# A two-branch attention kernel: three units of maxima, some weight casts and one value bank are moved

## The chip, the cores and the metric

The kernel runs on one core of a Trainium2 chip. The core has five engines that run side by side, each with its own queue that is worked through in order: TensorE (PE, matrix products; PEld is its loading of weights), VectorE (DVE), ScalarE (ACT), GpSimd (POOL) and SyncE (SP, which here issues all DMA transfers). Products land in PSUM, eight banks of 128 x 512 floats; everything else lives in SBUF or in device memory. The metric is device time of one execution, in microseconds (us); the profile numbers one execution from the start of its span.

## The reference, cut to what matters

The inputs are one sequence `x` of 2048 tokens with 448 features, and the weights of two attention branches with 16 heads of 28 features each.

```python
g = _sigmoid((x * gate_w).sum(-1, keepdims=True))
a = _A_ref(x, A_wqkv, A_w_phi, A_wo)
b = _B_ref(x, B_wqkv, B_wo)
return g * a + (1 - g) * b
```

Branch A is linear attention: queries and keys of each head are multiplied by `w_phi`, and their features are the softmax of the result beside the softmax of its negative. With `kv = phi_k^T v` and `z = sum(phi_k)`, the output is `(phi_q kv) / (phi_q z + 1e-6)`, times `wo`. Branch B is full softmax attention, `softmax(q k^T / sqrt(28)) v`, times its own `wo`.

## The kernel before, in words

Float32 products are made of rounded pieces: a tensor is kept as a high half (a cast on ScalarE) and a low half (raw minus high, on VectorE or GpSimd), and a product takes three passes: high by high, high by low, low by high. `split_weight` and `split_x` do the high half at once and put the low half into the list `lows`; `take_lows()` issues what is in that list. So the place of `take_lows()` sets where the low halves stand in VectorE's or GpSimd's queue. The order of each of PE, DVE, ACT and POOL is the order in which the code issues; only SP's queue is ordered by a scheduler.

The program has four parts.

Projection (iterations `n` = 4 to 19, about the first 63 us): `proj_qk` makes one 128 x 512 block of B's queries and keys in 11 passes, ScalarE and VectorE split it into `ev`, and SP writes it to memory (`qkd`). Here `x` is split (`XH`, `XL`), `wvA` is cast, and `fold` multiplies A's key weights by `w_phi`.

Key stage (`t` = 0 to 15, to about 181 us): for each 128 tokens A's key features (`pk`) and values (`pva`), and their product `pkv`.

Query stage (`q = i - 16`, from q = 0, about 181 to 324 us): for q up to 15, `pq` (11 passes), copied by ScalarE to `pcq`; `features1` takes minima and maxima on VectorE (`ext`), subtracts on POOL or VectorE (`featq`; for q = 4 and 6 the second subtraction, L431, is on VectorE) and ScalarE exponentiates; `features2` sums on VectorE and scales on POOL. Three iterations later `turn` transposes them on TensorE (`pft`) and ScalarE copies them to `fT`; every second iteration `numer` makes numerators and denominators (`pn`, copied to `oUa` on ScalarE). The normalization is spread over iterations: `normalize1` sends the denominators out by DMA (`dena`), `normalize2` takes the reciprocal on VectorE and sends it to memory and back, spread over the partitions (`rda`, then `rsa`), `normalize3` multiplies on VectorE (L400), `normalize4` casts to `oTa` (high on ScalarE, L408, low on POOL, L409). From q = 11 on, `out_a(t)` with t = q - 11 multiplies two `oTa` tiles by `woA` in 12 passes (`poa`), and `out_a2` scales by the gate (`ga`). `woA` itself is cast in this stage, high on ScalarE (L143), low on POOL (L144). From q = 18 on, `value_b` makes B's values (`pvb`).

Scores of B (about 363 us to the end): scores, exponentials and value products.

Spread over the first three parts are 80 *units of maxima*, `mx_unit()`: bounds of the scores of B's query rows. A unit is four matmuls of 28 rows into four PSUM banks (`pmd`, `pmb`), then twice a relu on ScalarE (L264) and a maximum on VectorE (L265, which the order calls ISA). Their banks form a ring of four (tag `mx`), so that a unit waits until the unit before it has been worked off by ScalarE (`pmd`) and VectorE (`pmb`). Units are numbered as they are issued; a few of them also ask for the next loads of rows (`qp`). In the query stage before, one stands in every iteration with q = 0, 1 and from 8 on, behind `pq`, and a second one in q = 19 to 25. Most other products take their bank from the ring `s` (four banks in the query stage, two from q = 22 on, where the maxima get six).

Of the kernel before, what the change touches and what calls it, by code (L numbers as in the profile page):

```python
# [17 lines left out]
P = 128  # L18
S = 2048
D = 448  # L20
# [3 lines left out]
NG = 4  # L24
# [17 lines left out]
def gated_mix_kernel(ctx, tc, xT, wqkB, wvB, wvA, wkAT, wqAT, phi, woA, woB,  # L42
# [7 lines left out]
    nc = tc.nc  # L50
# [56 lines left out]
    def run(dst, todo):  # L107
        for i, (l, r) in enumerate(todo):
            nc.tensor.matmul(dst, l, r, start=i == 0, stop=i == len(todo) - 1)  # L109
# [25 lines left out]
    lows = []  # L135

    def take_lows():
        while lows:
            lows.pop(0)()
# [98 lines left out]
    def mx_unit():  # L238

        u = mxs["u"]  # L240
        if u == NF:
            return
        mx_fin()
        mxs["u"] = u + 1
        gq, r = divmod(u, 16)
        g, qb = divmod(gq, NQ)
        c, qt = divmod(r, 4)
        hp, b = divmod(c, 2)
        col = 64 * gq + 16 * b + 4 * qt + 2 * hp
        if r in (4, 9) and gq + 1 < GM:  # L250
            pair_query(gq + 1, r // 9)
        if r == 4 and gq + 1 == GM:
            mx_query(GM)
        qc, kc = mxs[("qp", gq, hp)], mxs[("kp", g, c)]

        pm = [ps_mx(f"pm{'ddbb'[j]}{u}_{j % 2}") for j in range(4)]
        for j in range(4):
            i = (j + 2) % 4
            js = slice(32 * i, 32 * i + DH)
            nc.tensor.matmul(pm[j], qc[js, qt * P:(qt + 1) * P], kc[js, :], start=True, stop=True,  # L260
                             tile_position=(32 * i, 0))
        for i in range(2):
            rl = rlp.tile([P, 512], F32, tag="rl", name=f"rl{u}_{i}", bufs=psn[2])
            nc.scalar.activation(rl, pm[i], AF.Relu)  # L264
            nc.vector.tensor_tensor_reduce(rl, pm[2 + i], rl, 1.0, LOWEST, ALU.add, ALU.max,  # L265
                                           part[:, col + i:col + i + 1])
        if gq + 1 < GM and qt == 3 and qb == NQ - 1:
            pair_load(g + 1, c)
        if gq + 1 == GM and qt == 3:
            mx_load(GM // NQ, c)  # L270
        if r == 15:
            mx_reduce(gq)
# [53 lines left out]
    def split_x(t, raws):  # L326
        tt = slice(t * 512, (t + 1) * 512)
        if t == 3:
            for b, raw in enumerate(raws):
                nc.scalar.copy(XH[:, b, tt], raw)  # L330
                lows.append(lambda b=b, raw=raw: (nc.gpsimd if b == 2 else nc.vector).tensor_sub(
                    XL[:, b, tt] if b < 3 else XH[64:, 3, tt], raw[64 * (b == 3):],
                    f32(XH[64 * (b == 3):, b, tt])))
            return
        for b, raw in zip((0, 2), raws):
            nc.scalar.copy(XH[:, b:b + 2, tt], raw)

            def low(b=b, raw=raw):
                if b == 0:
                    nc.vector.tensor_sub(XL[:, 0:2, tt], raw, f32(XH[:, 0:2, tt]))  # L340
                else:
                    (nc.gpsimd if t > 1 else nc.vector).tensor_sub(
                        XL[:, 2, tt], raw[:, 0, :], f32(XH[:, 2, tt]))
                    nc.vector.tensor_sub(XH[64:, 3, tt], raw[64:, 1, :], f32(XH[64:, 3, tt]))

            lows.append(low)
# [66 lines left out]
    def out_passes(oT, c, w, g):  # L413
        tt = slice(c, c + P)
        return [(oT[:, 0, tt], w[:, 0, g, :]), (oT[:, 0, tt], w[:, 1, g, :]),
                (oT[:, 1, tt], w[:, 0, g, :])]
# [119 lines left out]
    def out_a(t):  # L536
        tb, tl = divmod(t, 2)
        po_of[t] = po = ps_s(f"poa{t}")
        run(po[:, :D], [x for g in range(NG)
                        for x in out_passes(oTs[tb][g % 2], g // 2 * 256 + tl * P, woA_s[:, :, :, :D], g)])  # L540

    def out_a2(t):
        ga = ta.tile([P, D], F32, tag="ga", name=f"ga{t}", bufs=3)
# [12 lines left out]
    def proj_qk(n, ev):  # L556

        m, t = UNITS[n]
        tt = slice(t * 512, (t + 1) * 512)
        pq = later.pop(0) if later else ps_s(f"pqk{t}_{m}")  # L560
        w, c = wB[m // 4], m % 4 * P
        run(pq, [(w[:, i, b, c:c + P], x) for b, x, i in x3(tt)])
        keep_qk(m, t, pq, ev)
# [30 lines left out]
    def splits(n):  # L594

        if n % 4 == 1 and n < 12:
            split_x(n // 4 + 1, raws.pop(("x", n // 4 + 1)))
        if n in (13, 15):
            split_part(wB[1], "wB1", 384, (n - 13) // 2)
        take_lows()  # L600
# [41 lines left out]
    for n in range(4, NP):  # L642
        take_acts()
        if n == 4:
            x_loads(2)
            raws[("x", 3)] = [load_last(b) for b in range(4)]
        if n == 8:
            nc.sync.dma_start(phi_s, phi)
            load_fold(wkAT, "k")
        if n == 10:  # L650
            part_loads("wB1", wqkB[:, :, 512:896], 384, "wB1")
        splits(n + 1)
        if n == 14:
            part_loads("wvA", wvA, 450, "wvA")
            nc.sync.dma_start(sel_s, sel)
            nc.sync.dma_start(mask_s, mask)
            for v in vap:
                nc.gpsimd.memset(v[:, :, 28:32], 0.0)
                nc.gpsimd.memset(v[:, :, 28:29], 1.0)
        if 16 <= n < 20:  # L660
            mx_unit()
        proj_qk(n, ev)
        if n in (17, 19):
            split_part(wvA_s, "wvA", 450, (n - 17) // 2)
            take_lows()
        if n in (13, 14, 15, 16):
            fold(wkA_s, "k", {13: 0, 14: 1, 15: 2, 16: 3}[n])
        if n == 10:
            pair_query(0, 0)
            pair_load(0, 0)  # L670
        if n == 15:
            pair_load(0, 1)
            pair_query(0, 1)
        if n in (14, 19):
            take_subs()
# [10 lines left out]
        return v  # L686

    def value_b(t, mid=None):
        pv = ps_s(f"pvb{t}")
        tok_major(pv, t, wvB_s, D, mid)  # L690
        nc.scalar.copy(vb[t // 8][:, t % 8, :, 0:DH], pv[:, :D].rearrange("p (h d) -> p h d", d=DH))

# [10 lines left out]
    for i in range(2 * NT + 11):  # L703
        t, q = i, i - NT
# [3 lines left out]
        if t < NT and t % 2 == 0:  # L708
            mx_unit()
            passes = (55 if t < NT - 4 else 44) + (4 if t >= 4 else 0)  # L710
            pace["n"], pace["at"] = 4 if t >= 4 else 0, [k * passes // 4 for k in range(1, 4)]
        if q in (0, 1):
            take_exps()
# [28 lines left out]
            fq[q - 1] = features2(fq[q - 1], f"q{q - 1}")  # L742
        if 0 <= q < NT:
            fq[q] = features1(pq, f"q{q}", nc.vector if q in (4, 6) else nc.gpsimd)
        if 0 <= t - 1 < NT - 1:
            fk[t - 1] = features2(fk[t - 1], f"k{t - 1}")
        if q in (0, 1) or q >= 8:
            mx_unit()
        if y >= 6 and y % 2 == 0 and tb - 3 < 8:
            num[tb - 3] = normalize2(ta, *num[tb - 3], f"a{tb - 3}", 2)  # L750
# [24 lines left out]
        if q == 2:  # L775
# [2 lines left out]
            for i in range(2):  # L778
                nc.sync.dma_start(raws["woA"][i], woA[:, 2 * i:2 * i + 2, :])
            part_loads("wvB", wvB, D, "wvB")  # L780
        if q in (4, 6):
            split_part(woA_s, "woA", D, (q - 4) // 2, nc.gpsimd)
        if q in (13, 15):
            split_part(wvB_s, "wvB", D, (q - 13) // 2)
        if q == 1:
# [458 lines left out]
```

## Time and profile before

| | us |
|---|---|
| three runs, median | 977.64 (976.87 to 979.13) |
| the profiled execution | 978.57 |
| its span (first to last instruction) | 976.8 |
| TensorE busy | 969.2 |
| ScalarE busy | 751.8 |
| VectorE busy | 715.7 |
| GpSimd busy | 227.8 |

The granted clock is 1.000 in the whole span. In a row of a timeline the first number is the start in us, the second the duration, then the engine, the line of the code, the operation, the tile written and those read, their shapes, and how often it was repeated; a bracket at the end is idle time of that engine ahead of it and what ended it. Matmuls overlap, so that the start of the next row, not the sum of the durations, gives TensorE's pace.

### The profile page before, as it was taken

How to read it: one execution, taken by the hardware profiler on the slowest of the kernel's cores; microseconds unless marked ns; L12 is line 12 of the kernel's file. 1: busy time of each engine (PE TensorE's matmuls, PEld its weight loads, DVE VectorE, ACT ScalarE, POOL GpSimd, SP SyncE). 2: the span in 40 equal slices, each digit the busy share in tenths (PEclk: the TensorE clock that was granted, in tenths of full speed). 3: DMA queues.
4: the chain of work that ended last, by engine and by line, in shares of the span. 5: the costliest groups of instructions: out<-in, count | busy, mean ns of one | idle time of the engine just before them, and what ended most of it. 6: DMA issues, size and time to landing. Idle time of an engine off the chain costs nothing.

```text
span 976.8 us, 22541 instructions
## 1 busy us (share of the span) xinstructions
PE 969.2 (99%) x8510; PEld 600.1 (61%) x8510; DVE 715.7 (73%) x1338; ACT 751.8 (77%) x1442; POOL 227.8 (23%) x236
## 2 busy tenths in 40 slices
PE   9999999999999999999999999999999999999998
PEld 8777877787777655555555555545555555555555
DVE  5567767788845678888888888888888888885112
ACT  4455655577865688989888898888988989887662
POOL 1135445577634800021001001011011011010010
PEclk9999999999999999999999999999999999999999
DMA  8873110023233333021132021122231222100441
GB/s 305 303 259 118 40 53 33 29 58 94 73 108 109 101 111 132 26 59 53 57 94 74 30 61 49 59 78 69 65 83 46 65 59 72 34 21 32 143 151 57
DMA packets 56140, 84.49 MB, mean 86 GB/s; under 512 B 17216, under 2 KB 23984, under 8 KB 56032
## 3 DMA queue, kind: packets, MB, share of 16 engines
q1 hardware_dynamic: 56032, 83.06, 27.1%
q8 instruction: 67, 1.10, 0.4%
q14 instruction: 41, 0.34, 0.1%
HBM read 54.86 MB, written 27.78 MB: 85 GB/s over the span
## 4 chain that ended last, share of the span: by engine, by line
PE 91%; DMA 5%; DVE 2%; ACT 1%; issue 1%; SPq 0%; DVEq 0%; ACTq 0%
PE g L863 29%; PE pv L1008 27%; PE pqk L109 4%; PE pk L127 4%; PE pva L127 4%; PE g L288 4%; PE poa L109 3%; PE pmd L260 3%; PE pob L109 3%; PE pq L109 3%; PE pvb L127 2%; PE pvb L109 2%; DMA rsa<-rda 2%; DMA qkd<-ev 1%; DMA xraw<-in_xT_dram 1%
## 5 line engine op out<-in xcount | busy, mean ns | idle before, releaser
L871 ACT ACTIVATE p<-g 128x512 f32<-128x512 f32 x1020 | 525.6, 608 | 82.7 <-PE g L863 82.4
L295 DVE TENSOR_REDUCE part<-g 128x1 f32<-128x512 f32 x704 | 442.3, 684 | 84.1 <-PE g L288 80.8
L863 PEld LDWEIGHTS g<-qst,kst 32*128 32x128 f32 x3060 | 220.9, 182 | 215.4 <-DVE part L295 195.1
L863 PE MATMUL g<-qst,kst 32*128 32x512 f32 x3060 | 337.6, 419 | 0.1
L1008 PE MATMUL pv<-p,vb 128*32 128x512 f32 x2048 | 273.0, 604 | 0.0
L288 PE MATMUL g<-kc,qc 28*128 28x512 f32 x704 | 233.3, 495 | 0.0
L265 DVE CUSTOM_DVE_ANT_0 rl<-pmb,rl 128x512 f32<-128x512 f32 x160 | 103.4, 683 | 49.6 <-ACT rl L264 49.6
L400 POOL TENSOR_TENSOR oUb<-oUb,rsb 128x512 f32<-128x512 f32 x15 | 19.3, 1289 | 489.9 <-DMA rsb<-rdb 366.2
L264 ACT ACTIVATE rl<-pmd 128x512 f32<-128x512 f32 x160 | 87.3, 601 | 31.1 <-PE pmb L260 29.3
L288 PEld LDWEIGHTS g<-kc,qc 28*128 28x128 f32 x704 | 86.2, 181 | 0.2
L1008 PEld LDWEIGHTS pv<-p,vb 128*32 128x32 f32 x2048 | 40.5, 108 | 66.2 <-issue 64.9
L109 PE MATMUL pqk<-XH,wB 128*128 128x512 f32 x192 | 59.4, 397 | 0.8 <-DVE ev L569 0.8
L568 ACT CAST ev<-pqk 128x512 fp32r<-128x512 f32 x28 | 16.0, 589 | 38.5 <-PE pqk L109 22.5
L1019 DVE SCALAR_TENSOR_TENSOR acc<-pob,gate,acc 128x448 f32<-128x448 f32 x12 | 8.2, 684 | 48.3 <-PE pob L109 48.3
L109 PE MATMUL poa<-woA_s,oTa 128*128 128x448 f32 x192 | 43.6, 375 | 0.0
L260 PE MATMUL pmb<-kp,qp 28*128 28x512 f32 x160 | 41.7, 495 | 0.4
L109 PEld LDWEIGHTS pqk<-XH,wB 128*128 128x128 f32 x192 | 35.3, 188 | 9.9 <-issue 1.5
L569 DVE TENSOR_TENSOR ev<-pqk,ev 128x512 fp32r<-128x512 f32 x28 | 18.9, 690 | 30.5 <-ACT ev L568 30.4
L260 PE MATMUL pmd<-kp,qp 28*128 28x512 f32 x160 | 39.9, 494 | 0.0
L127 PE MATMUL pk<-wkA_s,XH 128*128 128x448 f32 x128 | 39.4, 381 | 0.0
L109 PEld LDWEIGHTS poa<-woA_s,oTa 128*128 128x128 f32 x192 | 34.8, 188 | 6.6 <-issue 2.5
L109 PE MATMUL pq<-wqA_s,XH 128*128 128x448 f32 x128 | 37.3, 374 | 0.8 <-ACT oUa L381 0.8
(158 smaller groups left out, 1052.2 us busy)
## 6 DMA issues: line engine op xcount, KB each, us to landing
qkd<-ev SPq DMA_DIRECT2D x28, 512.0 KB
qst<-qkd SPq DMA_DIRECT2D x64, 112.0 KB
kst<-qkd SPq DMA_DIRECT2D x64, 112.0 KB
od<-oTb SPq DMA_DIRECT2D x48, 112.0 KB
rsa<-rda SPq DMA_DIRECT2D x8, 512.0 KB
oL<-od SPq DMA_DIRECT2D x8, 512.0 KB
rsb<-rdb SPq DMA_DIRECT2D x15, 256.0 KB
gad<-ga SPq DMA_DIRECT2D x16, 224.0 KB
```

The costliest lines, as they stand in the source:

```text
L109: nc.tensor.matmul(dst, l, r, start=i == 0, stop=i == len(todo) - 1)
L127: nc.tensor.matmul(dst[:, :n], l, r, start=i == 0, stop=i == len(todo) - 1, skip_group_check=True)
L260: nc.tensor.matmul(pm[j], qc[js, qt * P:(qt + 1) * P], kc[js, :], start=True, stop=True, tile_position=(32 * i, 0))
L264: nc.scalar.activation(rl, pm[i], AF.Relu)
L265: nc.vector.tensor_tensor_reduce(rl, pm[2 + i], rl, 1.0, LOWEST, ALU.add, ALU.max, part[:, col + i:col + i + 1])
L288: nc.tensor.matmul(pm, mxs[("qc", gq)][js, qt * P:(qt + 1) * P], mxs[("kc", gq // NQ, kb)][js, :], start=True, stop=True, tile_position=(3 ...
L295: nc.vector.tensor_reduce(part[:, col:col + 1], pm, AX.X, ALU.max)
L400: (nc.gpsimd if n == 1 else nc.vector).tensor_mul(oU, oU, rs)
L569: nc.vector.tensor_sub(e[:, 1, :], pq, f32(e[:, 0, :]))
L863: nc.tensor.matmul(st[j], kst_of[(gq // NQ, kt // 4)][js, k, (kt % 4) * P:(kt % 4 + 1) * P], qst_of[gq][js, q, :], start=n == 0, stop=n == ...
L871: nc.scalar.activation(p, st[j], AF.Exp, scale=SCALE)
L1008: nc.tensor.matmul(pv[32 * j:32 * j + 32, :], vb[kt // 8][:, kt % 8, 4 * g + j, :], pt[j], start=kt == 0, stop=kt == NT - 1, tile_position ...
```

## The change

Six small edits. In `split_x` the low half of the last block of `XH` goes to GpSimd. In iterations n = 16 to 19 the waiting low halves are issued behind the unit of maxima and ahead of the projection. The key stage issues them behind its first unit as well. `woA` is cast at the end of q = 3 and 4 instead of 4 and 6, and its first low half is issued within q = 4. The units of q = 8, 9 and 10 are left out there, and `out_a` issues one after its sixth pass for t = 1, 3 and 7 (q = 12, 14 and 18), so that from q = 19 on the numbers agree again. `value_b(4)`, the first after the banks are dealt out anew in q = 22, takes a bank of the maxima's ring; a bank of the ring `s` is passed over, so that the others stay where they were.

```diff
-                lows.append(lambda b=b, raw=raw: (nc.gpsimd if b == 2 else nc.vector).tensor_sub(
+                lows.append(lambda b=b, raw=raw: (nc.gpsimd if b > 1 else nc.vector).tensor_sub(
...
-        run(po[:, :D], [x for g in range(NG)
-                        for x in out_passes(oTs[tb][g % 2], g // 2 * 256 + tl * P, woA_s[:, :, :, :D], g)])
+        todo = [x for g in range(NG)
+                for x in out_passes(oTs[tb][g % 2], g // 2 * 256 + tl * P, woA_s[:, :, :, :D], g)]
+        for i, (l, r) in enumerate(todo):
+            if i == 6 and t in (1, 3, 7):
+                mx_unit()
+            nc.tensor.matmul(po[:, :D], l, r, start=i == 0, stop=i == len(todo) - 1,
+                             skip_group_check=True)
...
-        splits(n + 1)
+        if n < 16:
+            splits(n + 1)
...
         if 16 <= n < 20:
             mx_unit()
+            take_lows()
         proj_qk(n, ev)
         if n in (17, 19):
             split_part(wvA_s, "wvA", 450, (n - 17) // 2)
-            take_lows()
...
-        pv = ps_s(f"pvb{t}")
+        if t == 4:
+            ps_s("pvb_none")
+        pv = (ps_mx if t == 4 else ps_s)(f"pvb{t}")
...
             passes = (55 if t < NT - 4 else 44) + (4 if t >= 4 else 0)
+            take_lows()
...
+        if q == 4:
+            take_lows()
...
-        if q in (0, 1) or q >= 8:
+        if q in (0, 1) or q >= 11:
             mx_unit()
...
-        if q in (4, 6):
-            split_part(woA_s, "woA", D, (q - 4) // 2, nc.gpsimd)
+        if q in (3, 4):
+            split_part(woA_s, "woA", D, q - 3, nc.gpsimd)
```

On VectorE, iterations n = 17 and 18, before (`rl2` are the two maxima of unit 2, `ev` a projection's low half):

```order
L569 TENSOR_TENSOR ev1_4_586<-pqk1_4_574,ev1_4_586 128x512
L144 TENSOR_TENSOR wvA_s_116<-wvA_raw0_448,wvA_s_116 128x900
L265 ISA rl2_0_600,part_92<-pmb2_0_594,rl2_0_600 128x512
L265 ISA part_92 128x1
L265 ISA rl2_1_603,part_92<-pmb2_1_595,rl2_1_603 128x512
L265 ISA part_92 128x1
L569 TENSOR_TENSOR ev2_4_618<-pqk2_4_606,ev2_4_618 128x512
```

The same place after:

```order
L574 TENSOR_TENSOR ev1_4_586<-pqk1_4_574,ev1_4_586 128x512
L265 ISA rl2_0_599,part_92<-pmb2_0_593,rl2_0_599 128x512
L265 ISA part_92 128x1
L265 ISA rl2_1_602,part_92<-pmb2_1_594,rl2_1_602 128x512
L265 ISA part_92 128x1
L144 TENSOR_TENSOR wvA_s_116<-wvA_raw0_448,wvA_s_116 128x900
L574 TENSOR_TENSOR ev2_4_618<-pqk2_4_606,ev2_4_618 128x512
```

The low half of `wvA` moved from ahead of the two maxima to behind them.

On POOL, iterations q = 4 to 6, before (L429 and L431 are the subtractions of `features1`, L446 the scaling of `features2`):

```order
L429 TENSOR_TENSOR featq4_2391<-pcq4_2386,extq4_2388 128x16x28
L446 TENSOR_TENSOR featq3_2348<-featq3_2348,fsumq3_2395 128x16x28
L429 TENSOR_TENSOR featq5_2430<-pcq5_2425,extq5_2427 128x16x28
L431 TENSOR_TENSOR featq5_2430<-extq5_2427,pcq5_2425 128x16x28
L446 TENSOR_TENSOR featq4_2391<-featq4_2391,fsumq4_2434 128x16x28
L144 TENSOR_TENSOR woA_s_2295<-woA_raw0_2323,woA_s_2295 128x2x448
L429 TENSOR_TENSOR featq6_2494<-pcq6_2489,extq6_2491 128x16x28
```

The same place after:

```order
L429 TENSOR_TENSOR featq4_2392<-pcq4_2387,extq4_2389 128x16x28
L144 TENSOR_TENSOR woA_s_2295<-woA_raw0_2323,woA_s_2295 128x2x448
L446 TENSOR_TENSOR featq3_2348<-featq3_2348,fsumq3_2397 128x16x28
L429 TENSOR_TENSOR featq5_2432<-pcq5_2427,extq5_2429 128x16x28
L431 TENSOR_TENSOR featq5_2432<-extq5_2429,pcq5_2427 128x16x28
L446 TENSOR_TENSOR featq4_2392<-featq4_2392,fsumq4_2436 128x16x28
L144 TENSOR_TENSOR woA_s_2295<-woA_raw2_2324,woA_s_2295 128x2x448
L429 TENSOR_TENSOR featq6_2496<-pcq6_2491,extq6_2493 128x16x28
```

The first piece of `woA` moved up by one iteration, and the second piece took its old place.

On TensorE, the end of q = 12, before:

```order
L516 MATMUL pft9_4_2932<-ident_74,featq9_2655 128x128 x4
L109 MATMUL poa1_2943<-woA_s_2295,oTa0_0_2756 128x448 x3
L109 MATMUL poa1_2943<-woA_s_2295,oTa0_1_2759 128x448 x3
L109 MATMUL poa1_2943<-woA_s_2295,oTa0_0_2756 128x448 x3
L109 MATMUL poa1_2943<-woA_s_2295,oTa0_1_2759 128x448 x3
L109 MATMUL pq13_2959<-wqA_s_669,XH_87 128x448 x2
```

The same place after:

```order
L516 MATMUL pft9_4_2885<-ident_74,featq9_2641 128x128 x4
L544 MATMUL poa1_2896<-woA_s_2295,oTa0_0_2714 128x448 x3
L544 MATMUL poa1_2896<-woA_s_2295,oTa0_1_2717 128x448 x3
L260 MATMUL pmd40_0_2903<-kp0_2_655,qp2_1_1628 128x512
L260 MATMUL pmd40_1_2904<-kp0_2_655,qp2_1_1628 128x512
L260 MATMUL pmb40_0_2905<-kp0_2_655,qp2_1_1628 128x512
L260 MATMUL pmb40_1_2906<-kp0_2_655,qp2_1_1628 128x512
L544 MATMUL poa1_2896<-woA_s_2295,oTa0_0_2714 128x448 x3
L544 MATMUL poa1_2896<-woA_s_2295,oTa0_1_2717 128x448 x3
L109 MATMUL pq13_2926<-wqA_s_668,XH_87 128x448 x2
```

Unit 40, which stood in q = 10 before, now stands in the middle of the output product of t = 1. In q = 8, 9 and 10 the four matmuls between `pq` and what follows are gone.

## The prediction

> **What bounds the kernel now.** I read the page first, then TensorE's timeline (PE) for its idle brackets, then the timelines of the other engines at those brackets.
>
> ```profile
> span 976.8 us, 22541 instructions
> ...
> PE 969.2 (99%) x8510; PEld 600.1 (61%) x8510; DVE 715.7 (73%) x1338; ACT 751.8 (77%) x1442; POOL 227.8 (23%) x236
> ...
> PE 91%; DMA 5%; DVE 2%; ACT 1%; issue 1%; SPq 0%; DVEq 0%; ACTq 0%
> ```
>
> TensorE has work in 99% of the span and carries 91% of the chain that ended last. The change keeps every matmul, so the time can move only by TensorE's waits: some are taken away, some are made, and whatever is left at the end of the query stage reaches the end of the program, since nothing behind it has idle time to absorb it. I therefore go through the waits in order of time. A minus is time gained.
>
> **The waits in the first 70 us.** Part one moves one `XH` residue (rows 64 to 127 of block 3) from VectorE (DVE) to GpSimd (POOL).
>
> ```profile
> 33.21 0.72 PE L109 MATMUL pqk<-XH,wB 128*128 128x512 f32 x2 [0.83 <-DVE ev L569]
> ...
> 30.92 1.51 DVE L331 TENSOR_TENSOR XH<-xraw,XH 64x512 fp32r<-64x512 f32 x1 [0.18 <-ACT XH L330]
> 32.47 1.89 DVE L569 TENSOR_TENSOR ev<-pqk,ev 128x512 fp32r<-128x512 f32 x3
> ...
> 30.45 1.44 POOL L331 TENSOR_TENSOR XL<-xraw,XH 128x512 fp32r<-128x512 f32 x1 [8.90 <-ACT XH L330]
> ```
>
> TensorE waits for a bank that VectorE's `ev` subtraction frees; that one starts at 32.47 because the residue holds VectorE from 30.92. Without it the subtraction starts about 31.4 and TensorE goes on at its own pace: -0.83 by the bracket, up to -1.0 with the pipeline's restart. On POOL the residue follows the row at 30.45 and ends near 33.2; it is first read in the second projection unit after 33.21, some 2.5 us later, so it is covered there. The floor is no gain, if the DMAs behind that point hold TensorE instead. I take -0.9 (0 to -1.0), near the bracket because no row shows TensorE waiting for a DMA between 33 and 60.
>
> Part two puts the low halves of the `wvA` cast behind a unit of maxima on VectorE instead of ahead of it.
>
> ```profile
> 55.92 0.51 PE L260 MATMUL pmd<-kp,qp 28*128 28x512 f32 x2
> ...
> 56.36 0.73 PE L109 MATMUL pqk<-XH,wB 128*128 128x512 f32 x2
> ...
> 59.12 0.50 PE L260 MATMUL pmd<-kp,qp 28*128 28x512 f32 x2
> ...
> 60.34 0.73 PE L109 MATMUL pqk<-XH,wB 128*128 128x512 f32 x2
> ...
> 66.38 0.50 PE L260 MATMUL pmd<-kp,qp 28*128 28x512 f32 x2
> ...
> 67.50 0.47 PE L127 MATMUL pva<-wvA_s,XL 128*128 128x450 f32 x1
> ...
> 57.54 1.10 DVE L144 TENSOR_TENSOR wvA_s<-wvA_raw,wvA_s 128x900 fp32r<-128x900 f32 x1 [0.15 <-ACT wvA_s L143]
> ...
> 59.16 0.69 DVE L265 CUSTOM_DVE_ANT_0 rl<-pmb,rl 128x512 f32<-128x512 f32 x1
> ...
> 57.40 1.09 ACT L264 ACTIVATE rl<-pmd 128x512 f32<-128x512 f32 x2
> ```
>
> A unit that waits for nothing costs TensorE 0.44 us (55.92 to 56.36). The one at 59.12 takes 1.22 and the one at 66.38 takes 1.12: excess 0.78 and 0.68. Each wants a bank that the unit before it frees, and that unit's maxima stand behind 1.0 us of `wvA` work; the second maximum starts only at 59.16. With the cast behind it, it starts when ScalarE's relu is done (57.40 plus 1.09, so 58.5) and ends near 59.25: some 0.15 of wait is left in each place. I take -0.6 and -0.5 (together 0 to -1.4). The second cast half now starts as that bank is freed and ends 1.0 later; its first reader is the eighth value pass, 0.5 (restart, as at 67.50) and five passes of 0.2 behind the same moment: 0.5 of cover. Sum of the front: -2.0.
>
> **The query stage.** Up to the first output product the path is not TensorE's. Here is the chain of the first normalization, by engine.
>
> ```profile
> 209.87 1.97 POOL L144 TENSOR_TENSOR woA_s<-woA_raw,woA_s 128x896 fp32r<-128x896 f32 x1
> ...
> 210.56 1.77 DVE L431 TENSOR_TENSOR featq<-extq,pcq 128x448 f32<-128x448 f32 x1
> ...
> 214.81 0.34 DVE L389 RECIPROCAL dena<-dena 128x32 f32<-128x32 f32 x1
> ...
> 217.78 0.53 SPq L394 DMA_DIRECT2D rsa<-rda  x1
> 220.32 1.19 SPq L176 DMA_DIRECT2D qp<-qkd  x3
> ...
> 226.69 1.22 DVE L400 TENSOR_TENSOR oUa<-oUa,rsa 128x1024 f32<-128x1024 f32 x1 [1.98 <-DMA rsa<-rda]
> ...
> 227.94 1.14 ACT L408 CAST oTa<-oUa 128x512 fp32r<-128x512 f32 x2 [0.80 <-DVE oUa L400]
> ...
> 229.84 1.05 ACT L519 COPY fT<-pft 128x512 f32<-128x512 f32 x2
> ...
> 230.66 1.09 PE L529 MATMUL pn<-fT,KV 57*32 57x256 f32 x32
> ...
> 230.32 2.53 POOL L409 TENSOR_TENSOR oTa<-oUa,oTa 128x512 fp32r<-128x512 f32 x2
> ...
> 234.45 1.03 PE L516 MATMUL pft<-ident,featq 128*128 128x128 f32 x8
> ```
>
> VectorE sat idle 1.98 us for the `rsa` DMA and ScalarE 0.80 for VectorE. Behind the `oTa` casts in ScalarE's queue stand the `fT` copies that TensorE's `pn` needs, and the first output product needs POOL's low halves, which end at 232.85. So in this stretch the three units were filler: taking them out of q = 8, 9, 10 gives TensorE 3 x 0.44 = 1.3 us of lead, and it cannot spend it.
>
> ```profile
> 223.08 0.68 PE L109 MATMUL pq<-wqA_s,XH 128*128 128x448 f32 x2 [0.83 <-ACT oUa L381]
> ```
>
> The same holds for this wait of 0.83, which the thinner ScalarE queue and the earlier `woA` cast would remove, and for 0.6 of a unit's wait at 229.2: both lie ahead of `pn` and are worth nothing if `pn` waits. What counts is where the DMA chain ends, +x or -x against now, read at 234.45.
>
> Its start, the reciprocal at 214.81, stands in VectorE's queue behind L431, which took 1.77 beside POOL's `woA` piece and ended as that piece did. In the new order the other `woA` piece stands at the same place on POOL, ahead of `featq6`. The first piece moves one iteration forward and the two ScalarE casts (0.9 each) now stand ahead of the `fT` copies of q = 3 and 4, which delays TensorE there by 0.2 to 0.4 and VectorE's path likewise. I take +0.45 for the reciprocal (0 to +1.9, one whole `woA` piece). The `rsa` DMA itself: 217.78 to just before 226.69 is 8.8 us with `qp` loads beside it, which leave that stretch; the next one had almost none beside it:
>
> ```profile
> 227.87 0.53 SPq L394 DMA_DIRECT2D rsa<-rda  x1
> ...
> 236.11 1.74 DVE L400 TENSOR_TENSOR oUa<-oUa,rsa 128x1024 f32<-128x1024 f32 x1 [0.43 <-DMA rsa<-rda]
> ```
>
> That is 8.2, so -0.6 (0 to -0.6). Together -0.15 at 234.45, and the three units are still to be done.
>
> Beside that row a rule: the Trainium skill, page "SBUF — State Buffer", section "Who interferes with whom", says that VectorE with two SBUF inputs and GpSimd share one port pair, and that whichever issues first holds it for its whole instruction. By that rule the 1.77 is the wait for the rest of the 1.97, which agrees with the two rows; and were POOL's moved piece to issue ahead of VectorE's L431 of q = 4, the sum would be 979.7, the slower rival below, instead of 977.8.
>
> **The units in their new place.** Each adds its 0.44 (0.53 with the switch ahead of it, so 1.6 for three). It also comes soon after its iteration's own unit:
>
> ```profile
> 237.65 0.50 PE L260 MATMUL pmd<-kp,qp 28*128 28x512 f32 x2
> ...
> 238.93 2.71 PE L109 MATMUL poa<-woA_s,oTa 128*128 128x448 f32 x12
> 241.48 0.57 PE L109 MATMUL pq<-wqA_s,XH 128*128 128x448 f32 x2
> ...
> 239.99 0.69 DVE L265 CUSTOM_DVE_ANT_0 rl<-pmb,rl 128x512 f32<-128x512 f32 x1
> ```
>
> Twelve output passes take 241.48 - 238.93 = 2.55, six 1.28. The inserted unit so arrives 238.93 + 1.28 - 237.65 = 2.56 after the unit ahead of it, whose last bank VectorE frees at 239.99 + 0.69, 3.03 after. It waits 0.45. Queued behind it are the other six passes and the next `pq`. On ScalarE its two relus (1.09 in the row at 57.40) now stand ahead of the `ga` copy, which frees a bank that is not asked for until an iteration later; I cost that at nothing. The four `qp` loads that a unit releases come later on SP's queue, behind the third `rsa`, for a unit some ten units on: covered too. At t = 1 and 3 this pattern is the same. At t = 7 VectorE may be later:
>
> ```profile
> 272.39 1.23 DVE L400 TENSOR_TENSOR oUa<-oUa,rsa 128x1024 f32<-128x1024 f32 x1 [2.39 <-DMA rsa<-rda]
> ...
> 275.22 0.68 PE L109 MATMUL pvb<-wvB_s,XH 128*128 128x448 f32 x2 [0.18 <-ACT fT L519]
> ...
> 300.45 0.67 PE L109 MATMUL pvb<-wvB_s,XH 128*128 128x448 f32 x2 [0.34 <-ACT ga L544]
> ```
>
> There the maxima of the unit ahead stand behind L400, which waits for its own `rsa`; the `qp` loads leave that transfer too, so I take the same 0.45 (0 to 1.2). Three waits: +1.35 (0 to +2.1). In return the 0.18 at 275.22 is covered by the inserted unit, and the value bank moved to the maxima's ring takes away the 0.34 at 300.45: -0.5 (0 to -0.5).
>
> **Sum.** Front -2.0, chain -0.15, units +1.6, their waits +1.35, the last two waits -0.5: +0.3, rounded to +0.2 since the sizes are read to a tenth. The profiled execution took 978.57 (span 976.8 and 1.8 around it), 0.9 over the median of 977.64 of the three runs shown; the sum is a difference, so it is put on the median: 977.8.
>
> **Rivals.** *The lead is spent (faster).* If `pn` does not wait for the first normalization, TensorE keeps the 1.3 of the units, the 0.83 and the 0.6: 977.8 - 2.7 = 975.1. For it: VectorE's L431 could meet less of a POOL piece, the DMA loses its neighbours, and the inserted units may find their banks free. Against it: `rsa` would have to land 2.7 us sooner, where the rows give 0.6.
>
> *The port (slower).* POOL's first `woA` piece now stands between `featq4` and `featq3`, where VectorE has its half of `featq4` to do. If POOL is first, VectorE waits the 1.97 and everything behind it in its queue, the reciprocal included, is about 1.9 later: 977.8 + 1.9 = 979.7. It decides from the point at which POOL starts that piece before VectorE's L431 of q = 4 has begun. Against it:
>
> ```profile
> 211.80 1.33 POOL L429 TENSOR_TENSOR featq<-pcq,extq 128x448 f32<-128x448 f32 x1
> ```
>
> POOL's next instruction stood ready as its piece ended, and VectorE, which had waited longer, went first: L431 ended at 212.33 and this row took 1.33.
>
> *The front gives nothing (slower).* If DMA landings hold the front, the 2.0 are lost: 979.8. For it: the DMA share of the chain is 5%. Against it: the brackets of 33.21, 59.12 and 66.38 are on VectorE, and none of TensorE's up to 70 names a DMA.
>
> **Chances.** Less than 0.2% (about 2 us) can hardly be told from no change here. The balance 0.42 (own range 976.2 to 979.3); the spent lead 0.32; the port 0.14 and the front 0.12. So faster 0.32, same 0.42, slower 0.26. The range reaches a little beyond both rivals, 974.6 to 980.4, for waits that come together.
>
> **What the profile after would show.** Right: no bracket at 33.2, units at 59 and 66 near 0.6 long, an idle bracket of 2 to 3 us at the `pn` (or `poa`) of q = 11 ending with ScalarE or POOL, and pairs of units 2.6 us apart with a wait of 0.4. Wrong: no idle at that `pn` (the lead is spent), a `featq` L431 near 2 us at 204 to 206 (the port), or a new DMA bracket before 70.

## The result, and the profile after

The changed kernel takes 983.61 us in the median of six runs (981.88 to 985.70), the kernel before 978.00 beside it: a ratio of 1.0057, with a 95% interval of 1.0040 to 1.0074. It is slower by 5.6 us, and outside the forecast range. The profiled execution took 983.95 us, its span is 982.2. Two of the six runs had a mean granted clock of 1.000 and 0.999 and took 981.88 and 982.07 us, the other four had 0.995 to 0.998 and took 983.26 to 985.70.

The page of the changed kernel:

```profile
span 982.2 us, 22550 instructions
...
PE 971.7 (99%) x8510; PEld 602.5 (61%) x8510; DVE 715.5 (73%) x1337; ACT 751.9 (77%) x1442; POOL 230.6 (23%) x237
...
PE 95%; DVE 2%; DMA 1%; ACT 1%; issue 0%; SPq 0%; POOL 0%; DVEq 0%; POOLq 0%; ACTq 0%
```

TensorE's busy time grew by 2.5 us with the same 8510 matmuls: some of them have become longer. To find where the 5.4 us of span arose, I read the same instructions in TensorE's timelines of both profiles:

| instruction on TensorE | before | after | shift |
|---|---|---|---|
| first pass of `pq` for q = 0 | 181.21 | 179.82 | -1.39 |
| `pn` of q = 11 | 230.66 | 230.27 | -0.39 |
| `pft` behind the first output product | 234.45 | 235.46 | +1.01 |
| `pq` of q = 13 (behind the product of t = 1) | 241.48 | 243.49 | +2.01 |
| `pq` of q = 15 (behind the product of t = 3) | 254.83 | 257.90 | +3.07 |
| first `pvb` (behind the product of t = 7) | 275.22 | 279.49 | +4.27 |
| first scores `st` | 350.57 | 354.26 | +3.69 |
| first group of scores `g` | 353.10 | 357.80 | +4.70 |
| last output pass | 972.41 | 977.78 | +5.37 |

There are four places of loss: the stretch to q = 11, in which a lead of 1.39 us and three units of maxima left out gained almost nothing; the first output product; the moved units; and the first group of scores. Here are the first two, in TensorE's timeline of the changed kernel (L544 is now the output product's line):

```profile
225.95 0.50 PE L260 MATMUL pmd<-kp,qp 28*128 28x512 f32 x2
...
230.27 1.15 PE L529 MATMUL pn<-fT,KV 57*32 57x256 f32 x32 [3.82 <-ACT fT L519]
231.35 4.27 PE L544 MATMUL poa<-woA_s,oTa 128*128 128x448 f32 x12
235.46 1.04 PE L516 MATMUL pft<-ident,featq 128*128 128x128 f32 x8
```

The twelve passes and one window of 1 us in the kernel before:

```profile
231.68 2.93 PE L109 MATMUL poa<-woA_s,oTa 128*128 128x448 f32 x12
...
233.00:234.00 1.00, 1.00 (x5) 0.93 (x6) 1.00 (x5) 1.00 (x3) 1.00 (x2) 1.00 0.26 98
```

In the changed kernel TensorE idles for 3.82 us ahead of `pn`. Then the twelve passes take 4.11 us (231.35 to 235.46), where before they took 2.77 (231.68 to 234.45). The changed kernel's windows of 1 us there say why; in each row the number behind the five engines' busy times is TensorE's granted clock, then come the DMA share and GB/s:

```profile
231.00:232.00 1.00, 1.00 (x18) 0.61 (x3) 0.96 (x4) 1.00 (x4) 1.00 (x2) 0.74 0.33 111
232.00:233.00 1.00, 1.00 (x4) 0.87 (x4) 1.00 (x2) 1.00 (x3) 1.00 (x2) 0.50 0.25 102
233.00:234.00 1.00, 1.00 (x4) 0.91 (x3) 1.00 (x6) 0.92 (x2) 1.00 (x2) 0.50 0.26 106
234.00:235.00 1.00, 1.00 (x4) 0.87 (x3) 0.97 (x2) 0.00 (x0) 1.00 (x2) 0.55 0.05 20
235.00:236.00 1.00, 1.00 (x8) 0.90 (x8) 0.96 (x3) 0.34 (x1) 0.77 (x2) 1.00 0.16 15
```

The clock is at half for some 3.4 us; before it was 1.00 throughout. On the page this does not show, since one of its slices is 24 us wide and its mean stays above 0.9.

The hold itself is the chain of the first normalization, on SP, VectorE and ScalarE of the changed kernel:

```profile
217.02 0.54 SPq L394 DMA_DIRECT2D rsa<-rda  x1
...
226.50 1.22 DVE L400 TENSOR_TENSOR oUa<-oUa,rsa 128x1024 f32<-128x1024 f32 x1 [4.62 <-DMA rsa<-rda]
...
227.76 1.14 ACT L408 CAST oTa<-oUa 128x512 fp32r<-128x512 f32 x2 [4.27 <-DVE oUa L400]
...
229.65 1.05 ACT L519 COPY fT<-pft 128x512 f32<-128x512 f32 x2
```

L400 starts at 226.50 against 226.69 before. The chain hardly moved, and all that TensorE had gained ahead of it turned into waiting.

The moved units, in TensorE's timeline (in each group the last row is where the output product, or `pn`, goes on):

```profile
238.66 0.50 PE L260 MATMUL pmd<-kp,qp 28*128 28x512 f32 x2
...
241.35 0.88 PE L260 MATMUL pmb<-kp,qp 28*128 28x512 f32 x2
242.17 1.49 PE L544 MATMUL poa<-woA_s,oTa 128*128 128x448 f32 x6
...
255.76 0.89 PE L260 MATMUL pmb<-kp,qp 28*128 28x512 f32 x2
256.57 1.49 PE L544 MATMUL poa<-woA_s,oTa 128*128 128x448 f32 x6
...
260.49 1.11 PE L260 MATMUL pmb<-kp,qp 28*128 28x512 f32 x2
261.52 1.09 PE L529 MATMUL pn<-fT,KV 57*32 57x256 f32 x32
...
277.64 0.59 PE L260 MATMUL pmb<-kp,qp 28*128 28x512 f32 x2
278.16 1.49 PE L544 MATMUL poa<-woA_s,oTa 128*128 128x448 f32 x6
```

The units of t = 1 and 3 take 0.82 us each, that of t = 7 takes 0.52. The unit between, at 260.26, takes 1.26: its `pmb` wants the bank of the unit at 255.75, whose maxima on VectorE come behind a weight cast:

```profile
258.74 1.08 DVE L144 TENSOR_TENSOR wvB_s<-wvB_raw,wvB_s 128x896 fp32r<-128x896 f32 x1
259.74 0.68 DVE L265 CUSTOM_DVE_ANT_0 rl<-pmb,rl 128x512 f32<-128x512 f32 x1
```

And the first group of scores, which waited for nothing before (the first row is of the kernel before, the second of the changed one):

```profile
353.10 0.50 PE L863 MATMUL g<-qst,kst 32*128 32x512 f32 x2
...
357.80 0.50 PE L874 MATMUL g<-qst,kst 32*128 32x512 f32 x2 [0.94 <-ACT vb L699]
```

### The profile page after: what moved, and what is told of

Read it like the earlier page. It is cut to its first block, busy times and chain, and to the rows that moved or that the text cites. A ratio compares the mean times of both kernels' runs of the same rounds, so it can differ in the third digit from the quotient of the medians.

```text
span 982.2 us, 22550 instructions
## 1 busy us (share of the span) xinstructions
PE 971.7 (99%) x8510; PEld 602.5 (61%) x8510; DVE 715.5 (73%) x1337; ACT 751.9 (77%) x1442; POOL 230.6 (23%) x237
## 4 chain that ended last, share of the span: by engine, by line
PE 95%; DVE 2%; DMA 1%; ACT 1%; issue 0%; SPq 0%; POOL 0%; DVEq 0%; POOLq 0%; ACTq 0%
PE g L874 29%; PE pv L1019 26%; PE pqk L109 6%; PE poa L544 4%; PE pk L127 4%; PE pva L127 4%; PE g L288 3%; PE pmd L260 3%; PE pob L109 3%; PE pq L109 2%; PE pvb L127 2%; PE pvb L109 2%; PE pqk L635 1%; DMA rsa<-rda 1%; PE pft L516 1%; PE pkv L468 1%
## 5 line engine op out<-in xcount | busy, mean ns | idle before, releaser
L400 POOL TENSOR_TENSOR oUb<-oUb,rsb 128x512 f32<-128x512 f32 x15 | 19.3, 1289 | 494.4 <-DMA rsb<-rdb 462.4
L544 PE MATMUL poa<-woA_s,oTa 128*128 128x448 f32 x192 | 45.7, 386 | 0.0
L544 PEld LDWEIGHTS poa<-woA_s,oTa 128*128 128x128 f32 x192 | 35.9, 195 | 7.2 <-issue 3.7
L127 PE MATMUL pva<-wvA_s,XH 128*128 128x450 f32 x128 | 37.8, 371 | 0.0
```

Source lines behind the costliest of these rows:

```text
L127: nc.tensor.matmul(dst[:, :n], l, r, start=i == 0, stop=i == len(todo) - 1, skip_group_check=True)
L400: (nc.gpsimd if n == 1 else nc.vector).tensor_mul(oU, oU, rs)
L544: nc.tensor.matmul(po[:, :D], l, r, start=i == 0, stop=i == len(todo) - 1, skip_group_check=True)
```

## The experiments

My theory from the two profiles: the units cost by the hold and the lower clock behind it, and by being paid again later; the bank edit costs the 0.94 us at the first scores; the front gains. The rival: the lead is used and only the moved units' bank waits are paid, the rest of the loss being the casts'. All ratios are to the kernel before on the same chip, each with its 95% interval; an interval is 2 to 3 us wide, so differences of 1 us between two runs need their profiles as well. The first four runs make one part of the change each.

**The units alone.**

```diff
-        if q in (0, 1) or q >= 8:
+        if q in (0, 1) or q >= 11:
...
+            if i == 6 and t in (1, 3, 7):
+                mx_unit()
```

> Kernel before with one edit: the three units of maxima leave q = 8, 9, 10 and stand in the middle of the output products t = 1, 3, 7. Theory (the move itself costs, by a hold and a lower clock behind it): the lead of the missing units cannot be used, since the numerators of q = 11 wait for the features of the first normalization as before (they began at 230.66 us before and at 230.27 after the whole change); so TensorE idles there for about 3 to 4 us in place of the two waits of 0.83 and 0.6 us, its granted clock falls below 1.00 behind it and the output products of t = 0 take about 4.2 us in place of 2.8 (+1.4); three units in the new place cost 3 x 0.82 us and their own waits about 1.7 (0.39 + 0.39 + 0.8 + 0.1). Sum 1.4 + 2.5 + 1.7 = +5.6: about 983.5 us. Rival 1 (the lead is used, only the waits of the moved units are paid): +1.7, 979.7 us, clock 1.00. Rival 2 (the loss comes from the other edits): 978 us, within 0.5.

Measured: 981.78 us, ratio 1.0037 (1.0023 to 1.0052). TensorE's timeline and its windows of 1 us:

```profile
223.78 0.68 PE L109 MATMUL pq<-wqA_s,XH 128*128 128x448 f32 x2 [1.82 <-ACT oUa L381]
...
225.00:226.00 1.00, 1.00 (x5) 0.91 (x4) 0.02 (x1) 0.19 (x1) 0.84 (x1) 0.58 0.34 46
226.00:227.00 1.00, 1.00 (x4) 0.78 (x4) 0.86 (x1) 0.00 (x0) 0.10 (x1) 0.50 0.08 7
...
231.35 1.09 PE L529 MATMUL pn<-fT,KV 57*32 57x256 f32 x32
...
230.22 2.53 POOL L409 TENSOR_TENSOR oTa<-oUa,oTa 128x512 fp32r<-128x512 f32 x2
```

The units are the largest part, 3.5 us and not 5.6. The lead was lost here too: between the first `pq` and `pn` of q = 11 the three units left out gained 0.03 us in the profile. But the hold came in another form, a wait of 1.82 us ahead of `pq` of q = 10, then 3.4 us at half clock, and no wait at `pn`. So here the half clock filled a wait, though not wholly: TensorE came to `pn` 0.8 us after ScalarE's `fT` copies had ended (230.53). The `pft` behind the first output product starts 2.18 us after POOL's low halves end (232.75 to 234.93) and 1.60 before (232.85 to 234.45), so that by an estimate from these rows 0.6 of the 1.7 us of missing clock was paid. Rival 1, 979.7 us, and rival 2 are out.

**The front alone.**

```diff
-                lows.append(lambda b=b, raw=raw: (nc.gpsimd if b == 2 else nc.vector).tensor_sub(
+                lows.append(lambda b=b, raw=raw: (nc.gpsimd if b > 1 else nc.vector).tensor_sub(
...
-        splits(n + 1)
+        if n < 16:
+            splits(n + 1)
...
             mx_unit()
+            take_lows()
         proj_qk(n, ev)
         if n in (17, 19):
             split_part(wvA_s, "wvA", 450, (n - 17) // 2)
-            take_lows()
...
             passes = (55 if t < NT - 4 else 44) + (4 if t >= 4 else 0)
+            take_lows()
```

> Kernel before with the edits of the front alone: the lows of the fourth block on GpSimd, no splits from n = 16 on, the lows taken after each unit. Theory: in the whole change the first query projection began 1.39 us earlier (179.82 against 181.21 us); this gain is lost at the numerators of q = 11 only where the features are not earlier by as much, and the first reciprocal stood 0.77 us earlier there with the weight casts moved: so a gain of 0.6 to 1.4 us is left, 976.6 to 977.4 us, the idle time ahead of these numerators (0.60 us before) up by at most 0.8. Rival (the chain of the first normalization does not depend on TensorE's lead): all of it goes into that idle time, 978.0 us.

Measured: 977.01 us, ratio 0.9989 (0.9979 to 0.9998), a gain of 1.3 us, at the upper end of the theory. The rival is out: in its profile the first `pq` comes 0.68 us earlier than before and the reciprocal of the chain 0.69 (214.12), so the chain follows TensorE's lead where the casts do not hold it back. (The profiles of the units alone and of the bank alone, whose front is that of before, say the same: their first `pq` is 0.72 later and 0.72 earlier than before, their reciprocal 0.69 later and 0.73 earlier. So the 0.68 itself is within what this stretch scatters.) `rsa` was 0.8 shorter in this execution, too, and the wait at the unit of q = 11 shrank from 0.6 to 0.26; that of 0.83 at q = 10 stayed.

**The weight casts alone.**

```diff
-        if q in (4, 6):
-            split_part(woA_s, "woA", D, (q - 4) // 2, nc.gpsimd)
+        if q in (3, 4):
+            split_part(woA_s, "woA", D, q - 3, nc.gpsimd)
...
+        if q == 4:
+            take_lows()
```

> Kernel before with one edit: the two casts of the output weights at q = 3 and 4 in place of 4 and 6, and the lows taken at q = 4. Theory: ScalarE's share of the casts delays the query projections by 0.42 us between q = 0 and q = 7, and the first reciprocal of the normalization comes about 0.5 us later, so the features and the numerators of q = 11 come 0.3 to 0.8 us later: 978.3 to 978.8 us. Rival (the casts get out of the way of the reciprocals): the numerators come earlier and the waits of 0.83 and 0.60 us shrink, 977 us.

Measured: 979.40 us, ratio 1.0011 (1.0001 to 1.0021): slower by 1.1 us, more than the theory's 0.3 to 0.8, though the interval takes that in. In the profile TensorE is 0.38 later at `pn` of q = 5 than at the first `pq`, and 0.46 later at the end. Some 0.4 is shown; the rest of the median may be the scatter of such small differences.

**The value bank alone.**

```diff
-        pv = ps_s(f"pvb{t}")
+        if t == 4:
+            ps_s("pvb_none")
+        pv = (ps_mx if t == 4 else ps_s)(f"pvb{t}")
```

> Kernel before with one edit: the value projection of t = 4 takes a bank of the units' ring. Theory: the waits of 0.18 and 0.34 us ahead of two value projections (275.22 and 300.45 us of the trace of before) are not touched by it, or the second alone goes; and the order of the banks behind it is another, so that the first scores wait for the copy of the last values, 0.94 us as at 357.80 us after the whole change: +0.4 to +0.9, 978.4 to 978.9 us. Rival (the wait of 0.94 us comes from the lateness of the whole change and not from the banks): the second wait of 0.34 us goes and nothing comes for it, 977.6 us.

Measured: 979.18 us, ratio 1.0012 (1.0000 to 1.0024). Both small waits are gone, where the theory kept one or both (that of 0.18 is gone with the front alone, too, so only that of 0.34 is shown to go with the bank), and the new one is there with no other edit in the kernel:

```profile
353.54 0.51 PE L865 MATMUL g<-qst,kst 32*128 32x512 f32 x2 [0.91 <-ACT vb L693]
...
356.00:357.00 1.00, 1.00 (x10) 0.94 (x9) 1.00 (x3) 0.61 (x2) 0.00 (x0) 0.58 0.40 148
357.00:358.00 1.00, 1.00 (x9) 0.29 (x9) 0.40 (x2) 0.99 (x3) 0.00 (x0) 0.50 0.40 145
```

In this execution the clock fell behind the wait as well, for another 3.4 us. The rival, lateness of the whole change, is out.

Together the four parts make +3.5 - 1.3 + 1.1 + 0.9 = 4.2 of the 5.6 us. The other 1.4 would come from the parts together; it is no more than the intervals of the five ratios leave open.

**TensorE kept busy in the hold.** The changed kernel with sixteen passes more ahead of `pn` of q = 11, which write the bank that `pn` then overwrites:

```diff
+        for _ in range(16 if tb == 3 else 0):
+            nc.tensor.matmul(pn[0][:, :D], XH[:, 0, :P], wqA_s[:, 0, 0, :D], start=True, stop=True)
```

> The changed kernel with 16 more passes of 128 x 448 (a product of tokens and query weights, written to the bank of the numerators of q = 11 and overwritten there) ahead of these numerators, so that TensorE works through most of the 3.82 us in which it idled at 226.45 to 230.27 us. Nothing that the output needs is changed. Theory (the granted clock falls because TensorE idled): 16 passes at 0.20 us take 3.3 us, the idle time ahead of the numerators falls to about 0.5 us, the clock stays 1.00, the 12 passes of the output product of t = 0 take 2.8 us in place of 4.27: 1.4 to 1.7 us less than the changed kernel, about 982.0 us. Rival (the passes were slowed by something else at that time, transfers or the other engines): the 12 passes again take about 4.2 us, 983.6 us.

Measured: 982.17 us, ratio 1.0051 (1.0038 to 1.0064).

```profile
226.93 3.51 PE L526 MATMUL pn<-wqA_s,XH 128*128 128x448 f32 x16
230.63 1.15 PE L531 MATMUL pn<-fT,KV 57*32 57x256 f32 x32 [0.19 <-ACT fT L519]
231.71 3.07 PE L546 MATMUL poa<-woA_s,oTa 128*128 128x448 f32 x12
234.62 1.03 PE L516 MATMUL pft<-ident,featq 128*128 128x128 f32 x8
...
232.00:233.00 1.00, 1.00 (x5) 0.57 (x4) 1.00 (x3) 1.00 (x2) 1.00 (x2) 1.00 0.31 115
```

With 3.5 us of useless work added the kernel is 1.4 us quicker by the medians, 1.6 when each is set against the kernel before beside it; the intervals overlap, and the rows are the better evidence. The twelve passes take 2.91 us (231.71 to 234.62) with the other engines and the transfers as busy as in the changed kernel (GB/s 115 against 102). So the passes were slowed by the idle time ahead of them, through the clock, and the price in the changed kernel is 1.2 us by these rows and about 1.4 by the medians. The clock of the other executions agrees: the mean was below 0.999 in one of five here and in four of six of the changed kernel, whose other two, at 981.88 and 982.07 us, took what this one takes. The rest of the loss stands with the clock at 1.00.

**The units back, the other parts as changed.**

```diff
-        if q in (0, 1) or q >= 11:
+        if q in (0, 1) or q >= 8:
...
-            if i == 6 and t in (1, 3, 7):
-                mx_unit()
```

> The changed kernel with the three units of maxima back at q = 8, 9, 10; the front, the weight casts and the value bank as changed. Theory (the edits add up): front -1.3, casts +1.1, bank +0.9 by the medians of the runs of each alone: about 979.0 us, 4.6 us less than the changed kernel; no idle time above 1 us ahead of the numerators of q = 11. Rival (the hold is made by the casts and the lead of the front, whatever the units do): an idle time of 2 us or more there with a lower clock behind it, above 981 us.

Measured: 978.77 us, ratio 1.0006 (0.9993 to 1.0019): the parts without the units add up (-1.3 + 1.1 + 0.9 = +0.7, measured +0.6). The units so cost 4.8 us within the change and 3.5 alone. By the medians most of the difference is the clock: against the run with sixteen passes, which was timed on the same chip, they cost 3.4. What the idle time takes is only the lead: `pn` of q = 11 starts at 229.67 us here, with the three units worked off ahead of it, and at 230.27 in the changed kernel without them. These 0.6 are the `rsa` transfer, which took 8.85 us from issue to use in this profile and 9.48 in that one.

**The banks numbered anew.** The part of the front and the bank edit, and one more:

```diff
-    for i in (0, None, 1, 6, 5, 4, 3, 2):
+    for i in (None, 0, 6, 5, 4, 3, 2, 1):
```

This list says which of the eight banks is which of the score groups' (0 to 6) and which takes the attention's sums (`None`). In the kernel before the last values `pvb15` stood in the second bank, the one of the sums, which is needed late. The bank edit put them into the first, which the first score group writes at once, and turned the maxima's ring by one.

> Kernel before with the edits of the front and the value bank, and with one more edit: the banks of the attention stage are numbered so that the last values stand in the bank of the attention's sums, as in the kernel before, and the first group of scores takes banks that are free early. Theory (the wait of 0.91 us ahead of the first scores comes from the bank of the last values alone): the wait is gone, the waits of 0.18 and 0.34 us ahead of the value projections as well, clock 1.00: the front's 977.0 less 0.5, 976.5 us. Rival (that wait has another cause): it stays, 977.4 us or more.

Measured: 976.85 us, ratio 0.9987 (0.9978 to 0.9996). The first group of scores waits for nothing, and neither do the two value products:

```profile
351.72 0.50 PE L867 MATMUL g<-qst,kst 32*128 32x512 f32 x2
```

The wait came from the bank's number. This version is quicker than both kernels, but not to be told apart from the front alone (977.01).

**The units in the hold.**

```diff
         if q in (0, 1) or q >= 11:
-            mx_unit()
+            for _ in range(4 if q == 11 else 1):
+                mx_unit()
...
-            if i == 6 and t in (1, 3, 7):
-                mx_unit()
```

> The changed kernel with the three moved units not in the output products but one after the other at q = 11, ahead of the numerators, so that they stand in the 3.82 us in which TensorE idled. Theory (the loss is that the lead could not be used and the units had to be paid later): three units take 2.5 us and their bank waits inside the hold, the numerators begin at about 230.3 us as before, the clock stays near 1.00, and the 2.5 + 1.7 us of the units in the output products go: 983.6 - 1.4 - 4.2 = 978.0 us. Rival (the units' work on ScalarE and VectorE, three pairs of 1.09 us, stands ahead of the casts and copies that the numerators wait for): the numerators begin 2 to 3 us later, 980 to 981 us.

Measured: 987.67 us, ratio 1.0105 (1.0091 to 1.0118), beyond the rival's 980 to 981. TensorE, then ScalarE, then two windows of 1 us, the first with a lower clock and the last that is wholly at half:

```profile
230.81 1.28 PE L260 MATMUL pmd<-kp,qp 28*128 28x512 f32 x2 [3.82 <-ACT rl L264]
...
226.88 1.14 ACT L408 CAST oTa<-oUa 128x512 fp32r<-128x512 f32 x2 [2.85 <-DVE oUa L400]
...
230.14 1.11 ACT L264 ACTIVATE rl<-pmd 128x512 f32<-128x512 f32 x2
...
229.00:230.00 1.00, 0.00 (x0) 0.00 (x0) 0.98 (x1) 1.00 (x3) 1.00 (x2) 0.61 0.26 74
...
241.00:242.00 1.00, 1.00 (x4) 0.91 (x3) 0.00 (x0) 0.00 (x0) 0.63 (x1) 0.50 0.14 16
```

The idle time is still 3.82 us. A unit needs its predecessor's bank, that bank needs the relu on ScalarE, and the relu at 230.14 stands in ScalarE's queue behind the casts that wait for `rsa`. So the hold is one of ScalarE too, and what needs ScalarE cannot fill it; the three units then came on top of it, ahead of `pn`, at half clock, which lasted from 229.2 to 242.9. Both theories had units running during the hold, and both were wrong in that.

**One unit moved in place of three.**

```diff
-        if q in (0, 1) or q >= 11:
+        if q in (0, 1, 8, 9) or q >= 11:
...
-            if i == 6 and t in (1, 3, 7):
+            if i == 6 and t == 1:
```

> The changed kernel with one unit moved in place of three: the units of q = 8 and 9 are back, that of q = 10 stands in the middle of the output product t = 1. Theory (each unit taken out lengthens the hold by its own time and is paid again later; the clock falls once the hold is long): against the kernel with all three back (978.8 us) the idle time ahead of the first normalization's results grows by about 0.8 to some 1.7 us in two waits, the unit is paid at its new place with 0.39 us of wait: +1.2 us, 980.0 us with the clock at 1.00, and up to 1.7 us more in the executions in which it falls. Rival (the loss needs the long hold of three units, one unit's lead is used): 978.8 us as without units.

Measured: 979.34 us, ratio 1.0018 (1.0006 to 1.0029): 1.7 us over the kernel before, 1.1 more than without moved units, where the two intervals overlap. In the profile:

```profile
229.67 1.15 PE L529 MATMUL pn<-fT,KV 57*32 57x256 f32 x32 [1.05 <-ACT fT L519]
```

TensorE waits 1.05 us there, more than the 0.44 of the left-out unit, which so gained nothing. That `pn` starts at 229.67 as with all units back is chance: the first `pq` was 0.97 later and `rsa` 0.8 shorter. At the next `pn` the kernel is 1.24 later than that one (244.48 against 243.24): the theory's 1.2. The clock stayed at 1.00 behind these 1.05 us; in this execution (981.84 us) it was at half for 6.8 us behind the first scores' wait. Three units cost 4.8 us, one costs about 1.1.

**The units ahead of the output products.**

```diff
-            if i == 6 and t in (1, 3, 7):
+            if i == 0 and t in (1, 3, 7):
```

> The changed kernel with the three units ahead of the first pass of the output products t = 1, 3, 7 in place of the middle. Theory (the units' cost is their own time and the hold, not the place within the product): the waits of 0.39, 0.39 and 0.09 us change little or grow to about 0.8, since the unit before stands 1.4 us nearer: 983.6 to 984.8 us. Rival (the middle of the product is what costs): the waits go, 982.5 us.

Measured: 987.40 us, ratio 1.0104 (1.0088 to 1.0119).

```profile
238.22 0.71 PE L260 MATMUL pmd<-kp,qp 28*128 28x512 f32 x2
239.24 1.10 PE L260 MATMUL pmb<-kp,qp 28*128 28x512 f32 x2 [0.31 <-DVE part L265]
240.27 2.71 PE L544 MATMUL poa<-woA_s,oTa 128*128 128x448 f32 x12
```

A unit here takes 2.05 us (238.22 to 240.27) and not 0.82, at t = 7 it takes 2.03 and not 0.52: 1.2 + 1.2 + 1.5 = 3.9 us, about the difference to the changed kernel (3.8). The two profiles are only 2.8 us apart, since other things stand against it: `pn` of q = 11 came 0.7 earlier, the clock did not fall behind it, and the wait of 0.8 behind t = 3 is gone, while the clock fell for 3.4 us in the product of t = 7. Six passes between two units are worth more than the theory gave them, and the rival, that the middle is what costs, has the wrong sign.

## Why the prediction was wrong, point by point

- **What bounds.** Right: TensorE's waits decide, and what was left at the end of the query stage reached the end.
- **The front, -2.0.** Right in kind: no bracket at 33.2, and the units at 58.74 and 65.54 take 0.71 and 0.58 us as forecast. Too large: -1.39 in the profile, -1.3 by the run of it alone, and -1.0 over all twelve profiles (the first `pq` at 181.26 us in the mean of the four with the old front, at 180.29 in that of the eight with the new). The bracket of 0.83 at 33.21, priced at -0.9, was read from one execution: with the units alone it is 0.53, and with the casts alone, whose front is the same, there is none.
- **Chain and lead at `pn`: the step that failed first.** It said that TensorE cannot spend the units' lead, which the idle bracket of 3.82 us confirmed (2 to 3 were forecast; the unit at 229.21 takes 1.45 us, so that its wait is 1.0 and not 0.6 by the measure used at 59.12, and the front's lead goes into the bracket as well). But the sum put the front's -2.0 on top, as if the chain began earlier by all of it: -2.15 up to 234.45. The reciprocal came at 214.04, only 0.77 earlier: the casts had taken back 0.4, and L431 beside the other cast took 1.97 in place of 1.77. (Before, L431 did not end with POOL's piece, as I had read it, but 0.49 later, at 212.33 against 211.84.) Then `rsa` took 9.5 us from issue to use, where I had taken 0.6 off 8.8 for the loads that leave. In the profiles with these loads that stretch took 8.07 to 9.78, without them 7.65 to 9.48: the scatter is larger than what I subtracted. So `pn` was reached 0.39 and not 2.15 earlier, a miss of 1.8 us. How much of it is the transfer's scatter one profile cannot say. My own finding, that the lead is unusable, should have been applied to the front's share of it as well.
- **The clock: the term that was missing.** The profile of before had no idle bracket above 0.83 us in this stage and the granted clock 1.00, and I cost an idle time of 2 to 3 us at its length alone. What it did to the passes behind it was 1.4 us (4.11 against 2.77 for the product), of which 1.2 went with the idle time in the run with sixteen more passes.
- **The units in their new place, +2.95 with their waits.** The mechanism and the spacing were right (2.69 us apart, 0.39 waited against 0.45). Measured +3.3 (1.01 to 4.27): the unit of t = 7 waited 0.09 and not 0.45, but the unit behind that of t = 3 waited 0.8 for the bank that VectorE's cast of `wvB` held up. I had asked what the moved unit waits for, and not what the next one then waits for.
- **The bank, -0.5.** Both waits went, though that of 0.18 also goes without the edit. The price was the first score group's 0.94 us, more than 100 us later; I cost the edit by the waits that it takes away and did not ask which banks stand where at the next stage.
- **What stays open.** Between the first group of scores and the end the changed kernel lost 0.67 us more; 0.3 of it arose ahead of the first output product of B, 0.2 is a wait ahead of the last normalization. It was not followed up.
- **The rivals.** The port did not happen: VectorE's L431 of q = 4 started at 202.40 and took 0.87, and POOL's cast beside it, from 202.75, took 2.34. The spent lead did not happen. None of the three had what did, a loss behind the hold.

In sum: 1.8 us at `pn`, 1.4 by the clock, 0.5 with the units (+3.3 where the terms up to 275.22 made +2.8) and 1.4 behind the first value product (+1.1 where they made -0.3). Together these 5.1 us are what lies between the sum of +0.3 and the +5.4 of the profiles.

## What to carry to other kernels

Before filler is taken away from an engine that bounds the kernel, look for the next thing that it must wait for and that comes from a chain of its own: up to there the time saved is worth nothing, and work that needs the waiting engines cannot be put into the gap. Price idle time of TensorE at its length and add what the clock may cost the work behind it, by the granted clock in windows of 1 us and not by the page's slices. When a bank allocation is shifted by one, follow the numbers to the next stage that deals the banks out anew.

## What the runs showed of the hardware that was not expected

The granted clock fell to 0.50 for 3.4 us at a time, or a multiple of that. In the changed kernel's rows 0.26 + 0.50 + 0.50 + 0.45 = 1.71 us of clock are missing, which is 3.4 us at half; the same sum gives 3.4 with the units alone and with the bank alone, 6.8 with one unit moved and 13.7 with the units in the hold. It began 1.2, 1.4, 2.6 and 2.0 us after TensorE had gone on again in the first four, and 2.2 us into the idle time in the last. The idle times ahead were 3.82, 1.82, 0.91, 0.91 and 3.82 us. But 2.52 us (ahead of `pn` of q = 11 with the units ahead of the products) had no such stretch behind it in the profile, nor had the wait at the first scores in the other five profiles that show it (0.90 to 0.94, the changed kernel's among them). With the units ahead of the products there was one of 3.4 us from 279.5, behind a unit that had waited for its banks without an idle bracket. So the length of the gap alone does not decide, and what else does was not tried. The Trainium skill, page "TensorE: Matmul & The Clock Gate", section "Part 1: The HAM clock gate", says that the array's clock is halved after an idle window of about 3.4 us, that a busy window restores it, and that these windows run free of the program. The length of the stretches and their varying start agree with that; the stretches behind gaps of 1.82 and 0.91 us do not fit a gap of 3.4 us as the limit.

The times show it as well. Of the 65 executions of the kernel before that were timed beside the experiments, 59 had a mean granted clock of 1.000 or 0.999 over the span and took 978.0 us in the mean; six had 0.998, which is what one such stretch makes of it (1.7 of 977), and took 980.9. And the `rsa` transfer, 512 KB through memory, took 7.65 to 9.78 us from issue to use over the twelve profiles, hardly less without the neighbouring loads than with them.
